# Moving the stage reports of a staggered loop, and halving two output copies

## The chip, the core and the metric

One core of a Trainium2 chip runs the whole kernel. The engines are TensorE (PE; weight loads are listed apart as PEld), VectorE (DVE), ScalarE (ACT), GpSimd (POOL) and SyncE (SP), which computes nothing and issues most of the transfers. A name with a q behind it (SPq, ACTq) is the engine's instruction queue: waits, branches and the issue of transfers. The metric is the device time of one launch in microseconds (us), the median of several runs.

## The reference

`x` is 2048 tokens of 640 numbers. Two blocks run over it and are mixed by a gate per token, `g * a + (1 - g) * b`.

- Block B is attention over a window of 8 earlier tokens, two apart, with 32 heads of 20. It doesn't depend on block A and is done first.
- Block A is recurrent. The tokens are cut into 64 segments of 32. In each segment, 8 memory rows and the 32 tokens (40 rows, `h`) go through q, k and v projections (640 to 32 heads of 192), masked softmax attention over the 40 rows, and an output projection (6144 to 640). The first 8 output rows are the memory of the next segment, so the segments run one after another.

```python
h = concatenate([mem, xs])                 # 8 + 32 rows of 640
q, k, v = h @ Wq, h @ Wk, h @ Wv           # 32 heads of 192 each
p = softmax(mask(q @ k.T * scale))
o = (p @ v) @ Wo                           # 40 rows of 640
mem = o[:8]; outs.append(o[8:])
```

## The kernel before

Block B, then a pass that computes for all 64 segments the parts of q, k and v that don't depend on the memory (`prepass`), then the recurrence (`part_a`). The change lies in the recurrence alone. There each segment is written as two parts: "head" (the output rows of the segment before are finished and turned into the memory, and the first four blocks of q and k are computed) and "rest" (the last two q and k blocks, v, scores, softmax, values, output projection). Two heads and a rest stand ahead of the loop, one rest behind it; the loop of line 1017 runs 62 passes of rest and head.

**Weights.** Most weights stay in SBUF. The rest is streamed again in every pass: the 21 entries of `STREAM`, 15 of 256 KB (halves of q, k and v slices) and 6 of 192 KB (halves of output slices), through 7 slots `wst` of one entry each. In this document an entry is named by its place in `STREAM`, 0 to 20. Entries 0 to 5 are used in the head, 6 to 9 by `m_qk(4)` and `m_qk(5)`, 10 by `m_v(0)`, 11 and 12 by `m_v(1)`, 13 and 14 by `m_v(2)`, 15 to 20 by the output projection. SyncE issues the loads in that order. `release` (line 468) marks a slot as free when its last matmul has been written, and `pump` (460) then issues the load of the entry seven places on, which on the chip waits for that matmul. If `hold` is set, nothing is issued until the next `stage()` clears it and pumps.

**Stages and reports.** Instructions of the loop stand in four stages, cut by `stage()`: the first from the loop's top to line 946, the second to 978, the third to the head's line 904, the fourth to the loop's end. All engines are always in neighbouring stages: no engine enters a stage before every engine has reported that it is through with the stage before the last one. `done(engine)` says where in an engine's stream the report stands. Ahead of the report the engine waits until all that it issued in the previous stage is finished; for SyncE that means that its loads have landed. On entering a stage an engine resets the semaphores of the next one, one instruction each. All these instructions show up under line 1017.

`held()` is SyncE's report, and from there on loads are held back to the next stage:

```python
def held():
    done(SP)
    self.hold = True
```

Before the change SyncE reports in the first stage between `m_v(0, (0,1,2))` and `m_v(0, (3,4))`, in the second behind the load of entry 20 (released by `m_v(2, (0,1))`), in the third behind the output groups "oa", and in the fourth behind `c_qk(2)`, there without holding. The first report thus stands behind the loads of entries 14, 15 and 16, and the fourth behind entry 10, with 11 and 12 still to come.

**Around the output copies.** `o_group("oa")` sums 384 output columns in PSUM bank `psm0`, `o_group("ob")` the other 256 in `psm1`. VectorE copies them to `whi` (lines 999 and 1006). `pick("oa")` (889) turns three fifths of the copied rows into the transposed memory `hT`, behind group 9 of "ob", and the next head's `m_qk(0, (0,1,2))` needs that; `pick("ob")` does the rest in the head. Line 914 is a one-column VectorE write to `zst[0]`, which makes VectorE wait for GpSimd's store of that tile (654) before `c_qk(2)` overwrites it.

Of the kernel before, what the change touches and what calls it, by code (L numbers as in the profile page):

```python
# [27 lines left out]
class _K:  # L28
# [568 lines left out]
    def part_a(self):  # L597
        nc, tc, KC, S = self.nc, self.tc, self.KC, self.S
# [3 lines left out]
        with ctx:  # L602
            PP, KW, vz, sel, h_, a4 = self.work
# [4 lines left out]
            hT = h_[:].rearrange("p (c t) -> p c t", t=32)  # L608
            Es = [KW[:, f:f + 224].rearrange("p (a f) -> p a f", a=2) for f in (512, 0)]
            Vz = [vz[:, f:f + 128] for f in (0, 128, 256)]  # L610
            whi = KW[:, 0:640]
            xh = KW[:, 224:384]
            zst = [KW[:, 640:832], vz[:, 0:192]]
# [29 lines left out]
            def load_seg(s):  # L643
                nc.sync.dma_start(xh, row(self.xh_dram, s))
# [11 lines left out]
            def load_a4(s):  # L656
                nc.sync.dma_start(a4[:].bitcast(I32), self.bsc_dram[bass.ds(32 * s, 32)].rearrange("t j f -> j t f"))

            def tail():
                pa = Ss[0][:, 0, :]  # L660
                return pa, [nc.tensor.matmul(pa[32 * jj:32 * jj + 32, 0:160], lhsT=self.sel_x[:],
                                             rhs=whi[:, 160 * jj:160 * jj + 160], start=True, stop=True,
                                             tile_position=(0, 32 * jj), skip_group_check=True) for jj in range(4)]

            def mix(pa):
                nc.vector.scalar_tensor_tensor(out=a4[:, 0:160], in0=pa[:, 0:160], scalar=a4[:, 160:162].bitcast(F32),
                                               in1=a4[:, 0:160], op0=ALU.mult, op1=ALU.add)

            def store(s, last=False):
# [4 lines left out]
                else:  # L674
# [3 lines left out]
            PE, ACTE, DVE, SP, POOL = ALL = (mybir.EngineType.PE, mybir.EngineType.Activation, mybir.EngineType.DVE,  # L678
                                             mybir.EngineType.SP, mybir.EngineType.Pool)
# [3 lines left out]
            def segment(part, prev, s, nxt, looped=False):  # L683
                pSs = {}

                def stage(*engines):
                    if looped:
                        tc.stage_boundary()
                    done(*engines)
                    self.hold = False  # L690
                    self.pump()
# [5 lines that stand above are left out]
                def done(*engines):  # L697
                    if looped:
                        for e in engines:
                            tc.previous_stage_wait(e)  # L700


                def burst(ms):
                    if looped and len(ms) > 1:
                        key = ms[-1].ins.name
                        for m in ms[:-1]:
                            tc.no_tile_sem_insts.add(m.ins.name)
                            tc.add_to_no_dep_group(key, m.ins)
                        tc.declare_fence(ms[-1].ins, group=key)

                def m_qk(i, kcs):
                    p, m, pq = i // 2, "qk"[i % 2], pqs[i]
                    for kc in kcs:
                        sl = self.qk_columns((m, p, kc))
                        js = (2, 3, 0, 1) if (m, p, kc, 0) in STREAM else range(4)
                        burst([nc.tensor.matmul(pq[32 * j:32 * j + 32, :], lhsT=hT[:, kc, :], rhs=sl[j],  # L716
                                                start=(kc == 0), stop=(kc == KC - 1), tile_position=(0, 32 * j),
                                                skip_group_check=True) for j in js])
                        self.release(self.parts((m, p, kc)))

                def c_qk(i, part=None):
                    if part is None:
                        nc.scalar.copy(st[i], pqs[i])  # L723
                    elif part == 0:
                        nc.scalar.copy(st5[0], pqs[i][:, 0:256].rearrange("p (b x) -> p b x", b=4))
                    else:
                        nc.scalar.copy(st5[1], pqs[i][:, 256:512])

                def t_qk(i, part=None):

                    p = i // 2
                    if i % 2 == 0:
                        nc.vector.transpose(P[p][:, 1:5, :, :].rearrange("p b c i -> p c b i"), st[i])  # L733
                    else:
                        c0, c1 = (16 * p % 32, 16 * p % 32 + 16) if part is None else (8 * part, 8 * part + 8)
                        nc.vector.transpose(KT[:, c0:c1, :].rearrange("p c k -> p (c k)"),  # L736
                                            st[i] if part is None else st5[part])
# [70 lines left out]
                def m_v(t, kcs=range(KC)):  # L808
                    if t not in pvs:
                        pvs[t] = Ms[1 - t % 2]  # L810
                    for kc in kcs:
                        sl = self.v_columns(t, kc)
                        burst([nc.tensor.matmul(pvs[t][32 * j:32 * j + 32, :], lhsT=hT[:, kc, :],  # L813
                                                rhs=sl[j], start=(kc == 0), stop=(kc == KC - 1),
                                                tile_position=(0, 32 * j), skip_group_check=True)
                               for j in range(4)])
                        self.release(self.parts(("v", t, kc)))

                def c_v(t):

                    (nc.vector.tensor_copy if t == 0 else nc.scalar.copy)(Px[t], pvs[t][:])  # L821
# [45 lines left out]
                pso = {}  # L867
# [21 lines left out]
                def pick(part, pm):  # L889

                    m0, m1 = (0, 3) if part == "oa" else (3, KC)
                    p = 0 if part == "oa" else 1
                    burst([nc.tensor.matmul(pm[32 * jj:32 * jj + 32, p, 8 * (m - m0):8 * (m - m0) + 8],
                                            lhsT=whi[:, 128 * m + 32 * jj:128 * m + 32 * jj + 32],
                                            rhs=self.sel_m[:], start=(m == m0), stop=(m == m1 - 1),
                                            tile_position=(0, 32 * jj), skip_group_check=True)
                           for m in range(m0, m1) for jj in range(4)])
                    nc.vector.tensor_copy(hT[:, m0:m1, 0:8], pm[:, p, 0:8 * (m1 - m0)].rearrange(
                        "p (m i) -> p m i", i=8))

                if part == "head":
                    self.used = 0
                    m_qk(0, (0, 1, 2))
                    stage(POOL)
                    m_qk(1, (0,))
                    if prev is not None:
                        pick("ob", Ss[1])
                    m_qk(1, (1, 2))
                    if prev is not None:
                        pa, ms = tail()  # L910
                        burst(ms)
                    m_qk(0, (3, 4)); m_qk(1, (3, 4))
                    if prev is not None:
                        nc.vector.memset(zst[0][:, 0:1], 0.0)
                        mix(pa)
                    done(DVE)
                    c_qk(0); c_qk(1)
                    t_qk(0); t_qk(1)
                    m_qk(2, range(KC)); c_qk(2)
                    done(ACTE, SP)  # L920
                    t_qk(2)
                    m_qk(3, range(KC)); c_qk(3); t_qk(3)
                    done(PE)
                    return
# [6 lines left out]
                    store(prev)  # L931
                m_qk(4, range(KC))
                done(PE, ACTE, DVE)
                m_qk(5, (0, 1, 2))
                scores(0)
                m_qk(5, (3, 4))
# [1 line left out]
                c_qk(4); t_qk(4)  # L938
                c_qk(5, 0); t_qk(5, 0)
                c_qk(5, 1); t_qk(5, 1)  # L940
                m_v(0, (0, 1, 2))
                held()
                m_v(0, (3, 4))
                c_v(0)
                m_v(1, (0,))
                stage(POOL)
# [14 lines left out]
                if nxt is not None:  # L961
                    load_seg(nxt)
                    load_z(nxt)
                    load_a4(s)
                m_v(2, (0, 1))
                pairs = pv_half(0)
                e_sum(1)
                c_o(0, pairs)
                c_z(0, pairs, 1)
                m_v(2, (2,))  # L970
                held()
                m_v(2, (3, 4))
                e_norm(1)
                c_v(2)
                c_z(0, pairs, 0)
# [20 lines left out]
                for i2 in (6, 9, 7, 10, 8, 11):  # L996
                    o_group("oa", i2)
                held()
                nc.vector.tensor_copy(whi[:, 0:384], pso["oa"][:, 0:384])
                if nxt is not None:  # L1000
                    pm = X
                for i2 in range(4, 12):
                    o_group("ob", i2)
                    if i2 == 9 and nxt is not None:
                        pick("oa", pm)
                nc.vector.tensor_copy(whi[:, 384:640], pso["ob"][:, 0:256])

            ctx.enter_context(tc.manual_schedule(engines=set(ALL)))
            self.start_stream()
# [131 lines left out]
```

## Time and profile before

| what | value |
|---|---|
| median of 3 runs | 1661.0 us (1659.96 to 1664.59) |
| the profiled execution | 1660.96 us, span 1659.5 us |
| granted TensorE clock | 0.984 of full speed |
| PE busy in the span | 1505.6 us (91%) |
| DVE, ACT busy | 804.2 us, 666.3 us |
| HBM traffic | 267 GB/s over the span; 298 to 327 in the slices of the recurrence |
| the loop | 62 passes from 451.5 to 1571.4 us, 18.06 us each |

The recurrence is some two thirds of the time. In it PE is nearly always busy by its records, and the DMA engines too, so neither share tells what bounds a pass. What helps is to take one pass and to follow the waits: when a load is issued, when it lands, and when PE uses it. The times below that count from "zero" are medians or means over 55 passes of the loop, from the start of the first matmul on entry 6 (in `m_qk(4)`, just behind the loop's top). All instruction rows of the trace were used for them.

### The profile page before, as it was taken

To read this page: it belongs to the slowest core of one execution; us is meant where nothing else is said; L and a number is where in the kernel's file an instruction comes from. 1 tells how busy PE (TensorE), PEld (TensorE's weight loads), DVE (VectorE), ACT (ScalarE), POOL (GpSimd) and SP (SyncE) were. 2 spreads that over 40 slices of the span, in tenths; PEclk is the share of its full clock that TensorE was granted. 3 is DMA by queue.
4 is the path that set the end of the run, shared out by engine and by line. 5 is a ranking of instruction groups with operands and counts; after the bars stand their busy time and mean duration, and the time that the engine had idled before them with its cause. 6 is when DMAs were issued, how large, how long until landed. Compare 5 with 4: busy or idle time off the path is not lost. (4 is left out here: it accounts for less than half of the span.)

```text
span 1659.5 us, 91540 instructions
## 1 busy us (share of the span) xinstructions
PE 1505.6 (91%) x37462; PEld 858.0 (52%) x37477; DVE 804.2 (48%) x1999; ACT 666.3 (40%) x1609; POOL 143.6 (9%) x275
## 2 busy tenths in 40 slices
PE   6898898997689999999999999999999999999978
PEld 3455553443345555555555555555555555555547
DVE  4656542222245555555555555555555555555520
ACT  3765642222234443434434434443443443443430
POOL 4002000010000100010010010010010010000000
PEclk9999999999899999999999999999999999999989
DMA  6931049789879999999999999999999999999981
GB/s 161 214 112 54 30 132 286 185 197 274 269 252 321 304 323 298 312 307 327 309 311 320 320 303 313 317 306 317 324 310 322 317 315 315 319 307 317 313 205 28
DMA packets 438730, 438.32 MB, mean 264 GB/s; under 512 B 194172, under 2 KB 306820, under 8 KB 438660
## 3 DMA queue, kind: packets, MB, share of 16 engines
q1 hardware_dynamic: 344344, 395.02, 73.8%
q10 hardware_dynamic: 87148, 29.72, 7.4%
q0 software_dynamic: 7168, 12.60, 2.2%
q8 instruction: 51, 0.84, 0.2%
q14 instruction: 19, 0.16, 0.0%
HBM read 402.83 MB, written 39.48 MB: 267 GB/s over the span
## 5 line engine op out<-in xcount | busy, mean ns | idle before, releaser
L716 PEld LDWEIGHTS <-aH 128*32 128x32 bf16 x7680 | 208.6, 96 | 226.0 <-issue 41.5
L813 PE MATMUL psm<-wlate_v,aH 128*32 128x512 bf16 x3200 | 254.8, 380 | 4.5 <-DVE aP L821 3.5
L723 ACT CAST aP<-psx 128x512 bf16<-128x512 f32 x128 | 68.7, 589 | 330.2 <-PE psx L716 326.4
L716 PE MATMUL psx<-wlate_k,aH 128*32 128x512 bf16 x1920 | 198.7, 383 | 0.0
L876 PEld LDWEIGHTS <-aP 128*32 128x32 bf16 x6144 | 162.6, 96 | 59.9 <-ACT aP L855 18.9
L876 PE MATMUL psm<-wlate_oa,aP 128*32 128x384 bf16 x2560 | 167.3, 328 | 0.0
L736 DVE STREAM_TRANSPOSE aK<-aP 128x512 bf16<-128x512 bf16 (+1 forms) x256 | 142.7, 557 | 17.0 <-ACT aP L723 5.4
L716 PE MATMUL psx<-wst,aH 128*32 128x512 bf16 x768 | 138.4, 383 | 2.3 <-DMA wst<-wscr 1.9
L733 DVE STREAM_TRANSPOSE aP<-aP 128x512 bf16<-128x512 bf16 x128 | 91.1, 712 | 93.3 <-ACT aP L723 93.1
L813 PE MATMUL psm<-wst,aH 128*32 128x512 bf16 x640 | 125.2, 382 | 9.3 <-DMA wst<-wscr 8.1
L813 PEld LDWEIGHTS <-aH 128*32 128x32 bf16 x3840 | 93.6, 97 | 77.1 <-issue 14.1
L876 PE MATMUL psm<-wst,aP 128*32 128x384 bf16 (+1 forms) x896 | 128.7, 305 | 4.3 <-DMA wst<-wscr 4.3
L876 PE MATMUL psm<-wlate_ob,aP 128*32 128x256 bf16 x2688 | 126.0, 274 | 2.5 <-issue 2.5
L716 PE MATMUL psm<-wlate_q,aH 128*32 128x512 bf16 x1408 | 112.7, 382 | 14.6 <-PE psm L716 6.5
L716 PE MATMUL psx<-wres_q,aH 128*32 128x512 bf16 x1152 | 103.1, 388 | 10.1 <-ACT ZV L74 5.8
L776 DVE TENSOR_TENSOR aK<-aK,aSel 128x224 bf16<-128x224 bf16 x128 | 35.3, 276 | 158.8 <-ACT aK L775 157.6
L855 DVE CAST aP<-psx 128x128 bf16<-128x128 f32 (+2 forms) x192 | 75.5, 421 | 75.1 <-PE psx L843 75.1
L716 PE MATMUL psm<-wst,aH 128*32 128x512 bf16 x512 | 100.0, 381 | 2.3 <-SPq L1017 1.6
L855 ACT CAST aP<-psS 128x384 bf16<-128x384 f32 (+2 forms) x192 | 65.3, 375 | 88.2 <-PE psx L843 74.9
L775 ACT ACTIVATE aK<-psS 128x224 bf16<-128x224 f32 x128 | 46.1, 360 | 134.2 <-PE psS L767 134.2
L821 ACT CAST aP<-psm 128x512 bf16<-128x512 f32 x128 | 75.4, 589 | 49.9 <-PE psS L767 41.8
L716 PE MATMUL psm<-wlate_k,aH 128*32 128x512 bf16 x1024 | 86.5, 379 | 0.0
(165 smaller groups left out, 2725.2 us busy)
## 6 DMA issues: line engine op xcount, KB each, us to landing
wst<-wscr SPq DMA_DIRECT2D x965, 256.0 KB, 4.6
wst<-wscr SPq DMA_DIRECT2D x384, 192.0 KB, 3.7
aP<-zpk_dram SPq DMA_DIRECT2D x64, 192.0 KB, 3.3
zpk_dram<-ZS ACTq DMA_DIRECT2D x5, 2048.0 KB
aVz<-zpk_dram POOLq DMA_DIRECT2D x64, 96.0 KB, 4.0
wlate_k<-in_A_Wk_dram SPq DMA_DIRECT2D x8, 512.0 KB
wres_q<-in_A_Wq_dram SPq DMA_DIRECT2D x7, 512.0 KB
wst<-in_A_Wk_dram SPq DMA_DIRECT2D x14, 256.0 KB
```

The lines of the kernel that those rows point to most:

```text
L716: burst([nc.tensor.matmul(pq[32 * j:32 * j + 32, :], lhsT=hT[:, kc, :], rhs=sl[j], start=(kc == 0), stop=(kc == KC - 1), tile_position=(0, ...
L723: nc.scalar.copy(st[i], pqs[i])
L733: nc.vector.transpose(P[p][:, 1:5, :, :].rearrange("p b c i -> p c b i"), st[i])
L736: nc.vector.transpose(KT[:, c0:c1, :].rearrange("p c k -> p (c k)"), st[i] if part is None else st5[part])
L775: nc.scalar.activation(E, pSs[h][:, :, 0:112], ACT.Exp, scale=scale_a)
L776: nc.vector.tensor_tensor(out=E, in0=E, in1=self.mask[h].unsqueeze(1).to_broadcast([128, 2, 112]), op=ALU.mult)
L813: burst([nc.tensor.matmul(pvs[t][32 * j:32 * j + 32, :], lhsT=hT[:, kc, :], rhs=sl[j], start=(kc == 0), stop=(kc == KC - 1), tile_position ...
L821: (nc.vector.tensor_copy if t == 0 else nc.scalar.copy)(Px[t], pvs[t][:])
L855: (nc.scalar.copy, nc.vector.tensor_copy)[g](x.rearrange("p (j c q) -> p j c q", j=2, q=32), pairs[g][:, :, 0:240].rearrange("p j (c q) -> ...
L876: ms.append(nc.tensor.matmul(pso[part][32 * jj:32 * jj + 32, 0:n], lhsT=oT_slot(R // 2, j, 3 * (R % 2) + t), rhs=self.o_weights(osl, part, ...
```

## The change

- In the first stage, `held()` moves up from the middle of `m_v(0)` to behind `m_qk(4)`. The loads of entries 14, 15 and 16 are thereby held back to the second stage.
- In the second stage, `held()` moves up to behind the three loads of the segment (`load_seg`, `load_z`, `load_a4`). The load of entry 20 is held back to the third stage.
- In the fourth stage, ScalarE and SyncE report at the same place as VectorE, ahead of `c_qk(0)`, and SyncE now holds: the loads of entries 10, 11 and 12 are held back to the loop's top.
- The one-column write of line 914 goes to ScalarE (a copy from `hT`); VectorE instead writes zeros over `KW[:, 192:832]` behind `mix`.
- Each of the two copies to `whi` is split in two halves by columns; VectorE does the first, ScalarE the second.

```diff
@@ head
                     if prev is not None:
-                        nc.vector.memset(zst[0][:, 0:1], 0.0)
+                        nc.scalar.copy(zst[0][:, 0:1], hT[:, 0, 0:1])
                         mix(pa)
-                    done(DVE)
+                        nc.vector.memset(KW[:, 192:832], 0.0)
+                    done(DVE, ACTE)
+                    held()
                     c_qk(0); c_qk(1)
                     t_qk(0); t_qk(1)
-                    m_qk(2, range(KC)); c_qk(2)
-                    done(ACTE, SP)
-                    t_qk(2)
+                    m_qk(2, range(KC)); c_qk(2); t_qk(2)
@@ rest, first stage
                 m_qk(4, range(KC))
                 done(PE, ACTE, DVE)
+                held()
                 m_qk(5, (0, 1, 2))
...
-                m_v(0, (0, 1, 2))
-                held()
-                m_v(0, (3, 4))
+                m_v(0)
@@ rest, second stage
                     load_a4(s)
+                held()
                 m_v(2, (0, 1))
...
-                m_v(2, (2,))
-                held()
-                m_v(2, (3, 4))
+                m_v(2, (2, 3, 4))
@@ rest, third stage
                 held()
-                nc.vector.tensor_copy(whi[:, 0:384], pso["oa"][:, 0:384])
+                nc.vector.tensor_copy(whi[:, 0:192], pso["oa"][:, 0:192])
+                nc.scalar.copy(whi[:, 192:384], pso["oa"][:, 192:384])
...
-                nc.vector.tensor_copy(whi[:, 384:640], pso["ob"][:, 0:256])
+                nc.vector.tensor_copy(whi[:, 384:512], pso["ob"][:, 0:128])
+                nc.scalar.copy(whi[:, 512:640], pso["ob"][:, 128:256])
```

## The prediction

> **What bounds the kernel now.** I first read the page's busy lines and its list of transfers.
>
> ```profile
> PE 1505.6 (91%) x37462; PEld 858.0 (52%) x37477; DVE 804.2 (48%) x1999; ACT 666.3 (40%) x1609; POOL 143.6 (9%) x275
> DMA  6931049789879999999999999999999999999981
> ...
> wst<-wscr SPq DMA_DIRECT2D x965, 256.0 KB, 4.6
> wst<-wscr SPq DMA_DIRECT2D x384, 192.0 KB, 3.7
> ```
>
> PE and the transfers both look full all through the loop, so the shares don't settle it. A 256 KB entry lands 4.6 us behind its issue, a quarter of a pass of 18.06 us. Next come SyncE's own waits between 600 and 1600 us, some 55 passes:
>
> ```profile
> SPq L1017 <- DMA wst<-wscr: 59.9, 109, 1.5
> ```
>
> Line 1017 is the stage machinery: twice a pass SyncE's report waits for landings, 0.55 us on average, up to 1.5. In every pass and every stage but two cases SyncE reports last. Where does that stop PE? In one pass, instruction by instruction:
>
> ```profile
> L1017 SPq EVENT_SEMAPHORE  x7: 17/17/965, 1021.5 to 1023.4; - x7
> ```
>
> ```profile
> 1023.48 0.28 PE L791 MATMUL psS<-aK,aSel 128*32 128x160 bf16 x8 [1.11 <-DVE aK L736]
> ```
>
> The 965 ns (the last of 17/17/965) is the first stage's report, which waits for entries 11 and 12; it ends at 1023.18, and e_sum(0), the first matmul of the second stage, follows 0.30 later, with PE idle for 1.11. (The VectorE row that the view blames merely ended then; over the passes e_sum(0) follows the report by 0.29 to 0.32.) Left alone, e_sum(0) would come 3.54 us after zero; it comes at 3.94 on average, so this wait costs 0.40 us of PE a pass.
>
> A wait of PE is worth something only if nothing else sets the pass. So I looked at the head of the same pass: issue of entries 3, 4 and 5 (first three rows), their time to landing, and their first matmuls.
>
> ```profile
> 1010.63 0.40 SPq L464 DMA_DIRECT2D wst<-wscr  x1
> 1011.14 0.37 SPq L464 DMA_DIRECT2D wst<-wscr  x1
> 1011.61 0.37 SPq L464 DMA_DIRECT2D wst<-wscr  x1
> ```
>
> ```profile
> wst<-wscr SPq DMA_DIRECT2D x1, 256.0 KB, 4.7
> wst<-wscr SPq DMA_DIRECT2D x1, 256.0 KB, 5.5
> wst<-wscr SPq DMA_DIRECT2D x1, 256.0 KB, 5.6
> ```
>
> ```profile
> 1015.35 0.39 PE L716 MATMUL psm<-wst,aH 128*32 128x512 bf16 x2
> 1016.64 0.39 PE L716 MATMUL psm<-wst,aH 128*32 128x512 bf16 x2
> 1017.30 0.39 PE L716 MATMUL psm<-wst,aH 128*32 128x512 bf16 x2
> ```
>
> 1010.63 + 4.7 is 1015.33, the matmul starts at 1015.35; the next two fit as closely. The list of waits hardly shows this, as PE is then "idle" for less than a matmul's modelled length. Over 55 passes entry 3 is used within 0.1 us of landing in 35, entry 1 in 31. Chaining each pass's landings with the shortest gaps between uses reproduces when the head ends (correlation 0.98), and in that sum PE arriving 0.3 us later at the head moves its end by 0.02, landings 0.1 later by 0.10. So the head waits for loads, and a pass is as long as the way from one landing of entry 5 round to the next: report, first-stage loads, m_v(0) and m_v(1), SyncE's loads of the second stage, entry 0, and the landings behind it.
>
> **The change, part by part.** Zero is the start of the first matmul on entry 6. Before (medians, means for e_sum): entry 5 lands at -1.45; SyncE reports at -1.25; entries 10, 11, 12, 13 are issued at -2.21, -1.16, -0.68, 0.64, land at 1.92, 2.76, 3.53, 5.01 and are used at 2.89, 3.96, 4.62, 5.37; entry 19 is issued at 5.11, 20 at 7.55, the next entry 0 at 8.75, landing at 12.25.
>
> *Fourth stage.* SyncE's report stays tied to entry 5 (-1.25), but now entries 10, 11 and 12 stand behind the loop's top. The way from that report to a load is 0.96 us now (1018.35, end of one load, to 1019.31, start of the next), with 7 semaphores reset; the second stage would now issue 9 transfers, so two more resets of 0.065 each: 1.09. Entry 10 goes out at -0.16 (2.05 later than now), then 11, 12, 13 every 0.43 (0.27, 0.70, 1.13). When does 10 land? Entry 9 lands at 1.24, so the backlog is 1.4 us. Loads with 1.4 to 1.8 us of backlog took 3.50 (25 of them; quartiles 3.39 and 3.90, ends 2.96 and 4.25). I take 3.50, since GpSimd's 96 KB load of `aVz` is under way at that time: 3.34. m_v(0) wants it at 2.85, so PE stalls 0.49 there.
>
> *First stage.* SyncE's report now waits only for entry 9 (1.24), and comes at about 1.65 behind entry 13. e_sum(0) no longer waits for it: -0.40. But it follows entry 10's first matmul by 0.65: 3.34 + 0.04 + 0.65 = 4.03, against 3.94. The wait has changed places, +0.09. Entry 12 lands some 1.4 behind 10, at 4.75, and is wanted at 4.71: another 0.08. Entries 14 to 17 go out at 2.24 to 3.72 instead of 1.14 to 4.07, used from 7.08 on: no cost, the cover is over 1 us for each. SyncE then has entries 18 and 19 in front of the segment's loads as before, and PE's releases set them.
>
> *Second stage.* `load_seg` waits for scores(1), which end 1.51 behind e_sum(0) and 0.31 ahead of that load: 4.03 + 1.51 + 0.08 + 0.31 = 5.93, now 5.76. From it to entry 0 there are 3.02 us (1006.22 to 1009.24): three loads, entry 20, report, 7 resets. Without three of the resets, and a little less waiting, 2.77: entry 0 at 8.70, 0.05 earlier. But entry 20 now runs straight ahead of it (0.43) instead of 1.2 ahead. With 2.6 to 3 us of backlog a load took 3.66 instead of 3.50: landing at 12.36, +0.11. Entry 20 itself lands near 11.3, used at 11.28; what that costs lies beside the next item.
>
> *Halved copies.* By rows, VectorE's 128x384 takes 558 ns and 128x256 425, so 1.04 ns a column: 358 for 192. ScalarE's 266 (128) and 378 (256) give 322. Side by side the first copy ends 0.20 earlier; one after the other, with 0.05 between, 0.17 later. No row shows both engines reading one bank at once (the paired copies of line 855 read `psS` and `psx`), so I take 0.17 later and keep both ends. Either way it is covered: the head waits for loads, and 0.2 later costs 0.01 there. The cover is gone if loads come over 0.3 us earlier. The second copies end before pick("ob") needs them. The Trainium skill (page "PSUM — Partial Sum Buffer", section "PSUM bank collisions raise a hardware error") says that two engines must not touch one bank in the same partitions at once, reads included; by that the halves have to follow one another, and the sum at PE is +0.17, by a free reading -0.20. No run here shows it yet.
>
> *The rest.* VectorE's 640 columns of zeros: 325 ns by the 128x320 uint32 row, up to 0.67 at 1.04 a column; it fits in the 1.11 us that VectorE idles ahead of line 733's first transpose, which would be late otherwise. ScalarE's copy to `zst[0]` waits for the store of line 654 (issued 1009.50, median 3.9 to landing: 1013.4), and c_qk(0) is queued behind it at 1015.39: 1.5 us of room in the worst pass. ScalarE idles 4.92 us there, which takes its other copies too. GpSimd's queue issues the same as before.
>
> *Sum.* +0.11 us a pass; 62 passes: +6.8. The profiled execution took 1660.96 us (span 1659.5 and 1.5 around it), equal to the median within 0.1. That gives 1667.
>
> **Rivals.** (1) *Faster: the late loads keep up.* The point that decides is entry 10's landing at 2.85. With the shortest time seen, 2.96, it lands at 2.80, e_sum(0) comes at 3.54, and all behind it moves up 0.40; entry 0 lands 0.05 + 0.17 + 0.40 earlier, less some 0.2 for entry 20's 192 KB: about -0.4 a pass, 1636. For it: passes with a first-stage report ahead of 4.45 (from the branch) took 17.59 instead of 17.92. Against: 24 of those 25 loads took longer, and entry 13, with 2.9 of backlog in the same stretch, takes 4.37. (2) *Much slower: entry 10 is caught behind `aVz` and the output's store.* At 4.0 it lands at 3.84; +0.5 on everything that follows: +0.6 a pass, 1698. For it: entries 11 and 12 now scatter by 1 us in that stretch. (3) *No change:* SyncE's report still comes last and the waits swap evenly: 1661. In that case e_sum(0) would still start 0.3 behind a long line-1017 wait.
>
> **How the numbers follow.** My forecast, the waits change places with a small loss, 1667 (its own range 1661 to 1675): 0.45. Rival 1: 0.20, rival 2: 0.15, rival 3: 0.20. 0.3% is 5 us, about what a measurement of this kernel can tell from no change. Slower by more: most of the forecast (0.37) and rival 2, 0.52. Faster: rival 1 and the edges of rival 3, 0.27. Same: 0.21. For 8 in 10 the range leaves out the better half of rival 1 and the worse half of rival 2: 1640 to 1695.
>
> **What would show it.** In the profile after: line 1017's waits for `wst` on SyncE no longer end e_sum(0)'s idle time; instead line 813's matmuls on `wst` in m_v(0) start within 0.1 us of entry 10's landing. Entries 10 to 13 go out in one row 1 us behind SyncE's last wait. Entries 0 to 5 still land at their use. The ScalarE half of line 999 starts behind VectorE's. I'd be wrong if entry 10 lands before PE wants it, if the head stops waiting for loads, or if the halves or the report end on a wait I haven't named.

## The result, and the profile after

The changed kernel takes 1673.14 us (median of 7 runs, 1670.16 to 1677.83), the kernel before 1662.43 us (7 runs, 1659.96 to 1666.94): a ratio of 1.006, with a 95% interval of 1.0043 to 1.0076. It is slower by a little, on the side and in the range that the prediction gave. The profiled execution is the longest of the seven, 1677.83 us with a span of 1676.0 us, at a granted clock of 0.983.

The lines of the page that answer to those of before look nearly alike: PE busy a little longer, the transfers at the same density, the 256 KB entries landing somewhat sooner behind their issue (4.4 us, they were 4.6) and the 192 KB ones later (4.1, they were 3.7).

```profile
PE 1509.9 (90%) x37462; PEld 863.7 (52%) x37477; DVE 802.0 (48%) x1999; ACT 703.5 (42%) x1800; POOL 143.3 (9%) x275
...
DMA  6841049799889999999999998999999999999871
...
L813 PE MATMUL psm<-wst,aH 128*32 128x512 bf16 x640 | 126.0, 385 | 32.8 <-DMA wst<-wscr 31.3
...
wst<-wscr SPq DMA_DIRECT2D x965, 256.0 KB, 4.4
wst<-wscr SPq DMA_DIRECT2D x384, 192.0 KB, 4.1
```

One group of PE stands out: line 813, the v matmuls on streamed entries. PE idles 32.8 us ahead of them, nearly all of it for a landing; before it was 9.3 us, as the same line of the page of before shows:

```profile
L813 PE MATMUL psm<-wst,aH 128*32 128x512 bf16 x640 | 125.2, 382 | 9.3 <-DMA wst<-wscr 8.1
```

The waits of PE between 600 and 1600 us say so too (columns: total us, times, longest):

```profile
PE psm L813 <- DMA wst<-wscr: 21.0, 47, 1.5
PE psx L893 <- ACT aK L998: 10.9, 54, 0.2
```

The second of these is the wait for ScalarE's half of the "oa" copy, ahead of `pick`. Before, the longest in total was the one of e_sum(0); it is gone from the list:

```profile
PE psS L791 <- DVE aK L736: 10.7, 22, 1.1
```

In one pass, PE's rows give the place. Zero of this pass is 1005.87:

```profile
1009.40 0.27 PE L791 MATMUL psS<-aK,aSel 128*32 128x160 bf16 x8
...
1011.37 0.39 PE L813 MATMUL psm<-wst,aH 128*32 128x512 bf16 x2 [0.60 <-DMA wst<-wscr]
```

e_sum(0) (line 791) starts 3.53 behind zero with no wait ahead of it, where before it came at 3.9 behind SyncE's report. PE's wait behind that report is gone. (SyncE still waits for landings at its reports, 52.6 us in all between 600 and 1600 us, but the first report of this pass is through at 1007.83, long before e_sum(0).) In its stead PE stands at 1011.37, 5.50 behind zero, for the landing of entry 12. And the transfers in the 8 us from half a microsecond ahead of zero (40 slices of 0.2 us; busy share in tenths, GB/s), first of the kernel after:

```profile
DMA  9741007937998999999869999999999999999999
GB/s 399 277 174 51 31 20 51 61 102 266 328 463 330 351 371 398 391 195 215 154 246 318 369 338 389 338 338 338 382 346 371 366 361 359 333 376 399 407 376 369
```

and the same stretch of a pass of the kernel before, from 1000.13:

```profile
DMA  9999999898999999999999998986898779989756
GB/s 430 379 389 328 338 328 338 338 338 330 397 320 335 338 305 319 365 312 300 360 368 409 389 382 323 353 320 241 254 269 315 254 292 353 323 300 310 266 187 200
```

This is the main reading. Holding entries 10, 11 and 12 to the loop's top leaves the transfer engines with nearly nothing to do for 1.2 us (six slices of 20 to 102 GB/s; before, the same six show 328 to 338). What isn't moved there is missing at entry 12.

Taken over 55 passes (the same views, all rows; us behind zero, medians unless it says mean):

| | before | after |
|---|---|---|
| issue of entries 10 / 11 / 12 / 13 | -2.21 / -1.16 / -0.68 / 0.64 | -0.35 / 0.08 / 0.56 / 1.03 |
| their landing | 1.89 / 2.76 / 3.55 / 5.02 | 2.49 / 3.55 / 5.03 / 5.69 |
| e_sum(0), mean | 3.91 | 3.53 |
| first use of entry 12, mean | 4.67 | 5.04 |
| first use of entry 20, mean | 11.32 | 11.71 |
| first use of the next entry 0, mean | 12.68 | 13.12 |
| next zero (the pass), mean | 17.92 | 18.15 |
| passes of 55 with entry 12 used within 0.1 us of landing | 0 | 50 |
| next entry 0, from landing to first use, median | 0.25 | 1.03 |

So the kernel gains 0.38 at e_sum(0), is 0.37 behind at entry 12, 0.44 behind at the head's first entry, and the head gives 0.2 back: entry 0 now lands 1.03 us ahead of its use. What remains is 0.23 us a pass, 14 us over 62 passes, against 16.9 between the two profiled executions (and 10.7 between the medians: the profiled execution is the longest of its seven).

### The profile page after: what moved, and what is told of

Same layout as the page of the kernel before. It is cut to its first block, busy times and chain, and to the rows that moved or that the text cites. A ratio compares the mean times of both kernels' runs of the same rounds, so it can differ in the third digit from the quotient of the medians.

```text
span 1676.0 us, 91862 instructions
## 1 busy us (share of the span) xinstructions
PE 1509.9 (90%) x37462; PEld 863.7 (52%) x37477; DVE 802.0 (48%) x1999; ACT 703.5 (42%) x1800; POOL 143.3 (9%) x275
## 5 line engine op out<-in xcount | busy, mean ns | idle before, releaser
L716 PEld LDWEIGHTS <-aH 128*32 128x32 bf16 x7680 | 198.4, 96 | 210.6 <-ACT aK L723 36.2
L716 PE MATMUL psx<-wlate_k,aH 128*32 128x512 bf16 x1920 | 192.6, 384 | 0.0
L813 PEld LDWEIGHTS <-aH 128*32 128x32 bf16 x3840 | 99.0, 97 | 131.0 <-issue 69.1
L813 PE MATMUL psm<-wst,aH 128*32 128x512 bf16 x640 | 126.0, 385 | 32.8 <-DMA wst<-wscr 31.3
L716 PE MATMUL psm<-wlate_q,aH 128*32 128x512 bf16 x1408 | 108.4, 380 | 12.6 <-PE psm L716 2.6
L821 ACT CAST aP<-psm 128x512 bf16<-128x512 f32 x128 | 75.4, 589 | 96.2 <-PE psS L767 92.8
L716 PE MATMUL psx<-wres_q,aH 128*32 128x512 bf16 x1152 | 95.2, 386 | 8.9 <-ACT ZV L74 5.7
L723 ACT CAST aP<-psm 128x512 bf16<-128x512 f32 x128 | 74.6, 583 | 31.8 <-PE psm L716 31.8
```

## The experiments

I call the first stage's moved report A, the second's B, the fourth stage's part F (SyncE's report and the hold of 10, 11 and 12), and the halved copies H. The kernel after is A+B+F+H. All ratios are to the kernel before, with 95% intervals.

**F and the whole "oa" copy.** The kernel before with F; the "ob" copy is halved too, the "oa" copy whole. Line 914's write goes to ScalarE as in the kernel after.

```diff
...
-                    done(DVE)
+                        nc.vector.memset(KW[:, 192:832], 0.0)
+                    done(DVE, ACTE)
+                    held()
...
-                    m_qk(2, range(KC)); c_qk(2)
-                    done(ACTE, SP)
-                    t_qk(2)
+                    m_qk(2, range(KC)); c_qk(2); t_qk(2)
...
```

> The kernel before with the fourth stage's part alone: ScalarE and SyncE report ahead of c_qk(0), entries 10, 11 and 12 wait for the loop's top. (The copy of "ob" is halved too, since the early ScalarE report needs ScalarE to have waited for those matmuls; the copy of "oa" is whole, the first and second stage report as before.) Theory A, the late loads: after, entry 12 lands 5.02 us after zero and is used within 0.1 us in 50 of 55 passes, because 10 to 12 go out 2 us late; then this part alone gives the loss, ratio 1.004 to 1.010, and line 813 waits for wst. Theory B, the halves: the serial halves of "oa" make the memory 0.17 us late in each pass (10.5 us in all); then this kernel is at 1.000. Theory C, entry 20 in front of entry 0 delays the head's landings: 1.000 here as well.

Measured 1.010 (1.006 to 1.0141). PE waits in line 813 as in the kernel after:

```profile
PE psm L813 <- DMA wst<-wscr: 20.1, 46, 1.3
```

F, with half of H, is enough for the slowdown. e_sum(0) comes at 3.57, although SyncE's first report stands where it stood before: it now waits only for entry 9.

**All but F.** The kernel after with the fourth stage as before; VectorE's wide write of zeros stays.

```diff
...
-                    done(DVE, ACTE)
-                    held()
+                    done(DVE)
...
-                    m_qk(2, range(KC)); c_qk(2); t_qk(2)
+                    m_qk(2, range(KC)); c_qk(2)
+                    done(ACTE, SP)
+                    t_qk(2)
```

> The changed kernel with the fourth stage's part undone: ScalarE and SyncE report behind c_qk(2) as before and entries 10, 11 and 12 go out in the fourth stage; the earlier reports of the first and second stage and both halved copies stay. (VectorE's zeros over KW[:, 192:832] stay in place of the one-column write.) Theory A: no loss, 0.997 to 1.003, with e_sum(0) again 0.3 us behind SyncE's report, which again waits for entry 12's landing at about 3.5. Theory B: the whole loss, 1.006. Theory C: the whole loss, 1.006, with entries 1 to 5 landing 0.2 later than before and PE waiting for them.

Measured 1.0488 (1.0467 to 1.0509). Every theory fell. The trace shows why: entries 10 to 12 go out in the fourth stage again, so the early first report waits for entry 12 (lands at 3.53), and 14 to 17 are held behind it. Entry 14 goes out at 4.12 instead of 1.14, six loads stand ahead of the segment's first load (7.13 instead of 5.75, means), and entry 20 goes out at 9.49, used within 0.1 us of landing in 55 of 55 passes. Two later runs (A alone, B alone) take the moved reports apart.

**H alone.** The kernel before with both copies halved and the wide write of zeros; the cut shows the "oa" copy.

```diff
...
-                nc.vector.tensor_copy(whi[:, 0:384], pso["oa"][:, 0:384])
+                nc.vector.tensor_copy(whi[:, 0:192], pso["oa"][:, 0:192])
+                nc.scalar.copy(whi[:, 192:384], pso["oa"][:, 192:384])
...
```

> The kernel before with the two halved copies alone (and VectorE's zeros over KW[:, 192:832] in place of the one-column write, so that VectorE has waited for ScalarE's half ahead of its report); all reports and loads as before. Theory A: ScalarE's half still follows VectorE's, pick("oa") comes 0.17 us later, and that is hidden since the head waits for loads: 0.999 to 1.002. Theory B: 0.17 us in each of 62 passes, 1.006. Theory C: 1.000.

Measured 1.0014 (0.9997 to 1.0031): nothing. From entry 20's first use to entry 0's it takes 1.46 instead of 1.36 us, and the head, which waits for loads, takes that in: the pass is 17.95 against 17.92.

**The kernel after with the "oa" copy whole.**

```diff
-                nc.vector.tensor_copy(whi[:, 0:192], pso["oa"][:, 0:192])
-                nc.scalar.copy(whi[:, 192:384], pso["oa"][:, 192:384])
+                nc.vector.tensor_copy(whi[:, 0:384], pso["oa"][:, 0:384])
```

> The changed kernel with the copy of "oa" whole on VectorE again ("ob" stays halved). Theory A: after, the head waits less for loads than before (entry 0 lands 1.0 us ahead of its use, entry 5 0.35), so part of the 0.17 shows now: chaining the landings of after with PE 0.17 us earlier gives 0.04 to 0.05 us a pass, some 3 us: 1.003 to 1.005 against before. Theory B: 1.000. Theory C: 1.006.

Measured 1.0114 (1.0094 to 1.0135), not better than the kernel after but worse. From entry 20 to entry 0 it takes 1.22 us instead of 1.41, so one whole copy is 0.19 shorter than two halves, and that is lost in the head: entries 1, 3 and 5 are used within 0.1 us of landing in 27, 38 and 21 passes, in the kernel after in 18, 17 and 10. That explains no gain. The half per cent of loss isn't explained: in the profiled executions the pass is only some 0.03 longer than that of the kernel after, and entries 3 and 5 of the head land some 0.13 later for no reason that I found. Each of the two ratios was taken against runs of the kernel before made along with it; the two kernels were not run beside each other.

**Entry 10 kept in the fourth stage.** The kernel after with 11 and 12 held, 10 not.

```diff
-                    held()
                     c_qk(0); c_qk(1)
                     t_qk(0); t_qk(1)
-                    m_qk(2, range(KC)); c_qk(2); t_qk(2)
+                    m_qk(2, range(KC))
+                    held()
+                    c_qk(2); t_qk(2)
```

> The kernel after with one difference: SyncE's report and the hold of the fourth stage stand behind m_qk(2), so that entry 10 goes out in the fourth stage again (at about -2.2) and only 11 and 12 are held to the loop's top. Theory L (the loss is the queue of late loads: 11, 12 and 13 land one behind the other after 10): now 11 is the first one out at -0.35 and takes 2.9 as entry 10 did, landing at 2.5; 12 lands near 3.6 and 13 near 5.0, and only 13 is still at its use. e_sum(0) comes at 3.54 instead of 3.94, PE's stall on wst in line 813 goes from 0.5 us a pass to under 0.15. SyncE's first report now waits for entry 10 (lands 1.9), so entry 14 goes out at 2.6 to 2.9; no cost. Ratio to before 0.980 to 0.995. Rival T (the loads of a pass as a whole set its length, and an earlier m_v only waits longer further on): PE stops as long in the head, ratio 1.002 to 1.008 like the kernel after.

Measured 1.0002 (0.9985 to 1.002): better than the kernel after, short of the expectation. Entry 11, now the first held one, doesn't land at 2.5 as entry 10 did, but at 3.88: the gap has moved to between entries 10 and 11 (241 and 167 GB/s in the two half microseconds from 0.5 behind zero). `aVz`, issued at -0.33, is under way in it; whether it makes entry 11 late is not shown. e_sum(0) comes at 3.53, and PE then stands for entry 11 (45 of 55 passes) and 12 (46).

**Entry 12 alone held, the rest as before.**

```diff
-                    m_qk(3, range(KC)); c_qk(3); t_qk(3)
+                    m_qk(3, (0, 1, 2))
+                    self.hold = True
+                    m_qk(3, (3, 4))
+                    c_qk(3); t_qk(3)
```

> The kernel before with one difference: entry 12 alone is held from the fourth stage to the loop's top; reports and copies stay as before. Theory L: SyncE's first report waits for entry 11 (lands 2.76) instead of 12 (3.53), e_sum(0) comes at 3.54 to 3.6 instead of 3.94, entry 12 goes out at -0.35 and lands at 3.0, ahead of its use at 4.2; entry 17 and the segment's loads move up by 0.3 to 0.4. Ratio 0.978 to 0.992. Rival T: m_v is earlier by 0.4 but the head waits that much longer for its loads: ratio 0.997 to 1.003.

Measured 0.9853 (0.9837 to 0.987), 1638 us: faster than both kernels. The first report waits for entry 11 (lands 2.56) and e_sum(0) comes at 3.54. SyncE's waits at its reports have halved (before: 59.9 us, 109 times):

```profile
SPq L1020 <- DMA wst<-wscr: 28.4, 59, 1.1
```

and the late loads cost PE next to nothing:

```profile
PE psm L813 <- DMA wst<-wscr: 0.4, 2, 0.3
```

e_sum(0) comes 0.37 earlier, and the pass is 17.50, 0.42 shorter than before. That is the price of the first report's wait, measured: the head doesn't swallow it.

**The transfers of the first stage taken out.** The kernel after without `load_vz` and `store` in the loop: the memory's part of v and the stored rows of these passes are missing.

```diff
-                if prev is not None:
+                if prev is not None and not looped:
                     load_vz(s)
                     store(prev)
```

> The kernel after without two transfers of the loop's first stage: the load of aVz (GpSimd) and the store of the finished output rows (ScalarE) are left out in the 62 passes, so the memory part of v and the stored rows of these segments are missing. 136 KB a pass are not moved. Theory S (entry 12 is late because aVz and the store share the transfer engines with 11 and 12 just then): its latency falls from 4.46 to 3.4 to 3.9, it lands 0.5 or more earlier, the stall on wst in line 813 goes from 0.5 to under 0.2 us a pass, ratio to before 0.980 to 0.996. Theory Q (the stretch is slow because SyncE's queue had run empty, or because five loads start at once): the latency of 12 stays above 4.2, ratio 1.002 to 1.007.

Measured 0.9904 (0.9885 to 0.9923). Entry 12 lands at 4.49 instead of 5.03, and the wait goes:

```profile
PE psm L813 <- DMA wst<-wscr: 2.4, 7, 1.1
```

Half a microsecond is about what 136 KB take at 340 GB/s (0.41). The latency of 12, 4.00, lies a little over the 3.4 to 3.9 that I gave for contention and under the 4.2 of the rival; the gap is still there (88 to 119 GB/s in the first microsecond behind zero). So the gap is the hold's, and these two transfers lengthen what it costs. How much of their 0.6 us a pass (17.60 against 18.15) is owed to the gap isn't shown, since no run takes them out of the kernel before.

**B alone.** The kernel before with the second report moved.

```diff
                     load_a4(s)
+                held()
                 m_v(2, (0, 1))
...
-                m_v(2, (2,))
-                held()
-                m_v(2, (3, 4))
+                m_v(2, (2, 3, 4))
```

> The kernel before with the second stage's report alone moved up behind load_a4, so that entry 20 is held to the third stage. Theory A (in the run without the fourth stage's part the loss came from the first stage: its report waited for entry 12, six loads piled up ahead of the segment's loads): the second move by itself brings entry 20 from 7.55 to about 8.5, it lands near 11.3, just at its use; 0 to 0.1 us a pass, ratio 0.999 to 1.006. Theory B (the second stage's report was the seat of that loss): ratio 1.02 or more.

Measured 0.9979 (0.9955 to 1.0002): nothing. Entry 20 goes out at 8.14 instead of 7.55 and still lands 0.38 ahead of its use (median; in 16 of 55 passes within 0.1).

**Entry 12 held, and B.** The edits of the two runs together; the cut shows the lines added.

```diff
...
+                    self.hold = True
+                    m_qk(3, (3, 4))
...
                     load_a4(s)
+                held()
...
```

> The kernel before with two differences: entry 12 alone held to the loop's top, as in the run that gave 0.985, and the second stage's report moved up behind load_a4, as in the run that gave 0.998. Theory L: the two add up. The second one brings entry 0 out 0.2 earlier against the next zero (-9.25 instead of -9.07) and entry 20 some 0.5 later (7.7 instead of 7.2), landing at 10.5 to 10.7 for a use at 11.0; the head's waits on entries 1 and 3 get shorter: ratio 0.979 to 0.985. Rival: the head waits for the transfers' rate and not for their issue, or entry 20 comes late: 0.985 to 0.992.

Measured 0.9848 (0.9821 to 0.9875), 1635.6 us: the same as without B. Entry 0 is issued 0.15 and lands 0.56 earlier behind zero (means), but entries 1 and 3, which hold the head, do not (25 and 25 passes; 25 and 20 without B). The rival was right in its mechanism, though the ratio lies at the edge of the other's range.

**The kernel after with entry 12 alone held.**

```diff
-                    held()
                     c_qk(0); c_qk(1)
...
+                    m_qk(3, (0, 1, 2))
+                    held()
+                    m_qk(3, (3, 4)); c_qk(3); t_qk(3)
```

> The kernel after with one difference: the fourth stage's report and hold stand in m_qk(3), so that entry 12 alone is held to the loop's top; the first and second report stay moved up and the copies halved. Theory G (what costs in the kernel after is the gap that three held loads leave in the stream of transfers, 0 to 1.5 us behind zero; one held load leaves a third of it): entries 12 and 13 land near 4.0 and 5.0, the stall on wst in line 813 is under 0.1 us a pass, e_sum(0) comes at 3.6, ratio 0.984 to 0.994. Against it, what is left of the early first report: it waits for entry 11 (lands 2.6) with 14 to 17 held behind it, 14 goes out near 3.2 instead of 1.1 and the segment's first load near 5.9 instead of 5.4. Theory R (the early reports of the first and second stage cost as much as the hold): ratio 1.000 or more.

Measured 1.0119 (1.0078 to 1.0159). I expected a gain and got a loss; theory R, that the early reports cost as much as the hold, held. m_v is as good as hoped (entry 12 used at 4.44), but the early first report now waits for entry 11, with 14 to 19 behind it. Entry 14 goes out at 3.11, and entry 20, at 8.51, is used within 0.1 us of landing in 54 of 55 passes. The waits of PE have moved to line 876, the output projection:

```profile
PE psm L876 <- DMA wst<-wscr: 17.6, 35, 1.4
```

**A alone.** The kernel before with the first report moved.

```diff
                 done(PE, ACTE, DVE)
+                held()
                 m_qk(5, (0, 1, 2))
...
-                m_v(0, (0, 1, 2))
-                held()
-                m_v(0, (3, 4))
+                m_v(0)
```

> The kernel before with the first stage's report alone moved up behind m_qk(4), so that it stands ahead of entries 14 to 17 and they are held to the second stage. Theory A: entries 10 to 12 still go out in the fourth stage, so the report waits for 12 (lands 3.5); 14 goes out near 4.1, six loads pile up ahead of the segment's loads, which go out near 6.9 instead of 5.8, and PE waits about 0.7 us at the third stage for SyncE's second report. Ratio 1.035 to 1.055, as in the run without the fourth stage's part. Rival (the loss of that run needs the second report's move as well): 1.00 to 1.02.

Measured 1.0497 (1.0462 to 1.0533): the whole loss of the run without F is A's. SyncE's waits at its reports are two and a half times those of before, and PE stands ahead of line 837 at the third stage's entry, where it starts 0.29 us behind the end of SyncE's second report each time:

```profile
SPq L1016 <- DMA wst<-wscr: 146.9, 184, 2.3
```

```profile
PE psS L837 <- issue: 71.0, 52, 1.4
```

The transfers show the same kind of gap as F makes, longer and later. From 0.5 ahead of the zero of one pass:

```profile
DMA  9999888988978988997832111009907999982953
GB/s 399 420 369 338 266 307 307 358 307 307 348 300 330 328 222 279 321 397 295 294 112 73 61 41 51 0 0 102 123 31 276 379 402 366 384 307 108 184 92 100
```

From slice 21 on (3.5 behind zero) almost nothing moves for 2 us: entry 13, the last load issued, has been moved, and entry 14, issued only at 4.0, takes 2.67 to land.

**Entries 11 and 12 held, the rest as before.**

```diff
                     done(ACTE, SP)
+                    self.hold = True
                     t_qk(2)
```

> The kernel before with one difference: entries 11 and 12 are both held from the fourth stage to the loop's top; reports and copies stay as before. Theory G (each held load lengthens the gap in the stream of transfers behind zero): 11 goes out at -0.3 and lands near 4.0, as in the run that kept 10 with the early reports, 12 near 4.7 and 13 near 5.6. SyncE's first report no longer waits long, e_sum(0) comes at 3.6, but m_v(1) then stands for entry 11 until 4.0: what the report gives back is lost again. Ratio 0.994 to 1.003, between one held load (0.985) and three (1.010). Rival (holding loads helps as long as the report waits for none of them): 0.985 or less.

Measured 0.9953 (0.9927 to 0.9979), as expected. It completes a series in which A and B stay as before. The rates come from all packets of the trace, by half microseconds behind zero, mean of 55 passes:

| held | ratio | e_sum(0), mean | GB/s in 0 to 0.5, to 1.0, to 1.5, to 2.0 | entry 12 lands, median | its first use, mean |
|---|---|---|---|---|---|
| none (before) | 1 | 3.91 | 369, 342, 334, 346 | 3.55 | 4.67 |
| 12 | 0.985 | 3.54 | 374, 362, 325, 218 | 3.97 | 4.36 |
| 11, 12 | 0.995 | 3.52 | 366, 252, 203, 262 | 4.61 | 4.70 |
| 10, 11, 12 (F, H in part) | 1.010 | 3.57 | 152, 103, 225, 329 | 5.03 | 5.11 |

The first held load buys all of e_sum(0)'s 0.4 us; each further one only widens the gap. And the pass follows the first use of entry 12: its means in the four rows are 17.92, 17.50, 17.85 and 18.18, which is 13.25, 13.14, 13.15 and 13.07 behind that use, and 13.11 in the kernel after. In the runs in which the loads behind the early first report come late this no longer holds (A alone: 14.5).

## Why the prediction was right, point by point

The number was 1667 with 1640 to 1695, the measurement 1673: right in sign and in the range, and the forecast ("the waits change places with a small loss") is what happened. But the wait did not go where I put it, and the sum came out near by errors that partly cancel: that the number is so close is luck. (The sum's own terms give 1667.8.)

- *What bounds a pass.* Right for the kernel before. e_sum(0) stood behind SyncE's report, and that wait was worth 0.37 at e_sum(0) (3.91 to 3.54; I had 0.40) and as much of the pass: with entry 12 alone held, the pass is 0.42 shorter. My doubt whether the head would take it all in was unneeded, as SyncE's loads move up with PE (there entry 0 goes out at 8.38 instead of 8.75).
- *Fourth stage, issue times.* Right to 0.2: -0.35, 0.08, 0.56, 1.03, where I had -0.16, 0.27, 0.70, 1.13.
- *"I take 3.50 ... so PE stalls 0.49 there."* This term failed. Entry 10 takes 2.87 and lands at 2.49, ahead of its use in all but 4 passes. I took the latency from 25 loads with 1.4 to 1.8 us of backlog. All 25 are loads of entry 0, and between their issue and landing the engines moved some 920 KB; for entry 10 it is 680 KB. The backlog, the time until the load ahead lands, was as I had it (1.4), but it doesn't tell how many bytes are still to move. When entry 10 goes out, entries 7 to 9 haven't landed, but the rate is already falling, to 51 GB/s at 0.1 behind zero in the pass shown, since for some 2 us (from entry 9's issue at -2.83 to -0.35, less the 0.4 that one issue takes) SyncE has issued nothing.
- *"Entry 12 lands some 1.4 behind 10, at 4.75, and is wanted at 4.71: another 0.08."* This is the mis-sized term on the other side. It lands 2.5 behind 10, at 5.03. PE, ahead by 0.4 at e_sum(0), wants it at 4.28 (its median use where entry 12 alone is held), so it stands some 0.75 there. Of what I missed, 0.43 is the first error again (I had the entry wanted at 4.71, behind a stall that didn't come) and 0.28 is its later landing. In all I had entry 12's use 0.17 later than before; it is 0.37 later. What I left out is the gap: entry 13 used to go out at 0.64 behind three loads in flight; now 10 to 13 go out within 1.4 us behind an idle stretch. Against before, 316 KB are missing from 0 to 1.5 us ((369 - 128 + 342 - 72 + 334 - 213) GB/s by 0.5 us), 0.93 us at 340 GB/s. Entry 12 lands 1.48 later than before; what makes up the rest isn't taken apart.
- *First stage.* "Entries 14 to 17 go out at 2.24 to 3.72": 2.31 to 3.67, at no cost, as said. That A is free holds only because F leaves the report nothing to wait for but entry 9; I didn't see that A by itself costs 5%.
- *Second stage.* `load_seg` goes out at 6.10 (mean; I had 5.93), 0.35 later than before (5.75) and not 0.17. From there to entry 0 it is 2.78, before 3.02: 0.24 less, where I had 0.25. So entry 0 goes out 0.13 later and not 0.05 earlier. But it takes 3.22 to land (median) and not 3.66, and lands 0.19 earlier than before (12.20 against 12.39, means) instead of 0.11 later. My base was off too: the 12.25 that I had for before is 12.41 in the median over the passes, and against that my own terms give 0.05 less.
- *Sum.* Its last step failed: I let the pass move as entry 0's landing does. That landing came 0.19 earlier, and the pass is 0.23 longer. The head's first use is 0.44 later because PE gets there later, with entry 0 long landed; entries 1, 3 and 5 go out 0.29 to 0.39 later and land 0.13 to 0.19 later (means). The head gives 0.2 back, and the transfers run at 350 to 380 GB/s from 5 to 7.5 us, where before they had 270 to 300.
- *Halved copies.* Right. They follow one another, and two halves take 0.19 longer than one copy (I had 0.17 against whole copies), hidden by the head: H alone costs nothing. ScalarE's half waits for VectorE's in all 55 passes:

```profile
ACT aK L998 <- DVE aK L997: 89.4, 55, 1.6
```

  By the rule of the Trainium skill (page "PSUM — Partial Sum Buffer", section "PSUM bank collisions raise a hardware error") they had to; the trace agrees.
- *The rest.* Right: the write of zeros takes 0.33 us where I had 325 ns. ScalarE's copy waited for the store in 3 of 55 passes, 0.6 us in all.

```profile
1002.53 0.33 DVE L916 MEMSET aK<- 128x320 uint32 x1
```

- *Rivals.* Rival 1 named entry 10's landing at 2.85 as the point that decides. It landed at 2.49, and e_sum(0) moved up as that rival said, but the kernel didn't become faster: the point was set on the wrong load, the one that a hold delays least. Rival 2's mechanism may be real in part, for entry 12 and not for 10: without `aVz` and the store entry 12 lands at 4.49 instead of 5.03. Rival 3 is out: line 1017's waits no longer stand ahead of e_sum(0).
- *What would show it.* I named m_v(0)'s use of entry 10 within 0.1 us of landing; it is 4 passes of 55, and 50 for entry 12 (28 for entry 11 and 37 for entry 13). The head still waits for loads, but less: entries 3 and 1 are used within 0.1 us of landing in 17 and 18 passes, before in 35 and 31. I said that I would be wrong if entry 10 landed ahead of its use. By the mechanism I was, by the time not.

Open is the half per cent between the kernel after and its twin with a whole "oa" copy.

## What to carry to other kernels

When a load is held back, cost the stretch in which nothing is under way and not only the held load's own lateness: the missing bytes show at the later loads behind the gap. A queue's report should come when its own latest transfers have long landed; put ahead of loads that it then holds back, it turns its wait into theirs. Parts of such a change can hide one another's price (A alone 5% slower, with F next to nothing), so measure each alone, and look for the smallest part that takes the wait away: here one held load out of three, 1.5% faster, where the whole change lost 0.6%.

## What the runs showed of the hardware

- A 256 KB load issued into an idle stream (entry 14 in the run with A alone): 0.96 us from issue to its first packet and 2.67 us to landing (median of 55; the shortest 2.50), against 4.52 for the same load in the kernel before, where the stream is full. The Trainium skill (page "DMA: Bandwidth & Descriptors", section "Anatomy of one DMA — SWDGE (gpsimd) path") gives about 2.0 us and the bytes at 436 GB/s, an estimate of 2.60 for this size; the trace agrees for the idle stream, on SyncE's queue too.
- A gap in the stream isn't made up at once: in the kernel after the rate from 1.5 to 3 us behind zero is 336, 359 and 326 GB/s by half microseconds, in the kernel before 346, 342 and 328. Only from 5 to 7.5 us does it rise to 350 to 380, where the kernel before moves 270 to 300.
